# Attention scores as three float32r products from tile 4 on, and tile 1's probabilities split in float16

## The chip, the cores and the metric

The kernel runs on one core of a Trainium2 chip. The metric is the device time of one execution in microseconds (us); the kernel before takes 676.44 us, the median of three runs (675.19 to 678.43).

## What is computed

Attention with rotary embedding over 4 batches, 8 heads, 576 positions and head size 64, and then a two-layer network on the 2304 resulting rows of 512. All arrays are float32.

```python
q_rot, k_rot = rotate(q), rotate(k)
scores = matmul(q_rot, k_rot.T) / sqrt(64)
attn = exp(scores - max(scores))
attn = attn / (sum(attn) + 1e-09)
x = matmul(attn, v)                      # to [2304, 512]
h = x @ w_in                             # w_in [512, 2048]
g = maximum(h, 0) + alpha * minimum(h, 0)
out = g @ w_out                          # w_out [2048, 512]
```

## The kernel before, in words

The 2304 rows are cut into 18 tiles of 128 rows. 576 is four and a half tiles, so tile 4 and tile 13 hold the end of one batch and the start of the next, and each of these two is worked as two halves of 64 rows; the 16 others are whole. Two tiles make a block; there are nine blocks. Heads are worked in pairs (4 pairs a tile), since two heads of 64 fill the 128 partitions. The second layer stage that a block goes through is called an expert here: 16 steps j, each of a first-layer product of 128 columns of `w_in` (`l1`, into the buffer `h`), a leaky relu in two instructions (ACT, then DVE: the tile `r`) and a second-layer product (`l2`).

For a pair of heads, `pair` (L624) issues the scores on TensorE (PE) into two PSUM buffers, `pair`. Whole tiles use the two halves of the PE array, rows 0 to 63 for one head and 64 to 127 for the other. `half_pair` (L650) handles the two split tiles: it puts both heads' queries on a diagonal, `qd`, and uses the whole array. Then `head` (L680) takes the row maximum on DVE (`mx`), the exponential with its sum on ACT (`e`), and goes one of two ways:

- tiles 0 and 1 (`t < PRM["pf"]`, which is 2): `head_f32` (L733) turns the probabilities on PE with products by the identity (L745), copies them out of PSUM and multiplies by v in float32 (L751).
- all others: the probabilities are split into a float16 high part (`pp`, on ACT L707 or DVE) and a float16 rest (DVE L716), both are transposed by a DMA on the SP queue (L720, `pt<-pp`), and 14 float16 products follow (L727).

`keys` (L381) and `queries` (L602) load and rotate: a product with a table and a sum on POOL or DVE, into `ks` and `qn`. The weights come as 64-bit words. `weights` loads them on the SP queue into `wraw` (L529), and DVE turns each of 16 chunks into float32 by three instructions (L511, L516, L520). Blocks 0 and 1 run the expert in float32 (L817, L843); from block 2 on the first layer is three float16 products (L823) and the second three float32r products of split operands (L861).

The program writes nothing in the order of execution. Each operation is put in a list with a priority, its possible engines and a cost for each, and `Plan.run` deals the list out to the five engines ahead of time; the order, the engine and the buffers that come out of it are fixed in the program. The table `PRM` holds the offsets of the priorities. Each engine then works its instructions strictly in that order. SP's queue holds all loads and all DMA transposes, so an instruction there that waits holds up those behind it.

Of the kernel before, what the change touches and what calls it, by code (L numbers as in the profile page):

```python
# [9 lines left out]
F32 = mybir.dt.float32  # L10
F32R = mybir.dt.float32r
# [3 lines left out]
ACTF = mybir.ActivationFunctionType  # L15
# [36 lines left out]
class Tag:  # L52
    def __init__(self, pool, bufs, shape, dt, name, tag=None):
        self.pool, self.bufs, self.all, self.opened = pool, bufs, [], 0
        self.make = lambda: pool.tile(shape, dt, name=name, tag=f"{tag or name}{self.opened % bufs}")

    def new(self):
        k = len(self.all)
# [182 lines left out]
def attention_moe(ctx: ExitStack, tc: tile.TileContext, q, k, v, w_in, w_out, alpha, tab, eye, out):  # L241
# [64 lines left out]
    ks_T = tag("ks", PRM["nks"], [128, S], F32)  # L306
# [4 lines left out]
    qn_T = tag("qn", 2, [128, NP, 128], F32)  # L311
    st_T = tag("st", 2, [128, NP], F32)
    e_T = tag("e", 2, [128, S], F32)
    pp_T = tag("pp", 3, [128, 2, S], F16)
# [61 lines left out]
        small(at, lambda: nc.vector.reciprocal(out=dst(), in_=dst()), writes=[dst_acc])  # L376


    ks = {}

    def keys(at, b, p):  # L381
        r, t = rk_T.new(), ks_T.new()
        ks[b, p] = t
# [8 lines left out]
        op(at - PRM["ka"], {POOL: t_pool(S), DVE: (t_dve(S), slow)},  # L392
           lambda e: ENG[e].tensor_tensor(out=t(), in0=r()[:, 0], in1=r()[:, 1], op=ALU.add),
           reads=[(r, 0), (r, 1)], writes=[t])

# [204 lines left out]
    qs = {}  # L600

    def queries(at, t):  # L602
        raw, qn = qr_T.new(), qn_T.new()
        qs[t] = qn
        parts = tiles[t]
        cuts = [[0], [2]] if t == 0 else [[0, 2]]
        op(at - (PRM["qd0"] if t == 0 else PRM["qd"]), {SP: t_dma(128 * 2 * NP * 128 * 4)}, lambda e: nc.sync.dma_start(out=raw(), in_=q[t]),
           writes=[(raw, (p[2], x)) for p in parts for x in (0, 2)])
        for n, xs in enumerate(cuts):
            c, w = slice(xs[0], xs[-1] + 2), 2 * len(xs) * 128  # L610
            late = at - PRM["qa"] + 0.1 * n
            for b, s, a, z in parts:
                m = w * (z - a) // 128
                op(late, {POOL: t_pool(2 * m), DVE: (t_dve(2 * m), PRM["qr"])},
                   lambda e, s=s, a=a, z=z, c=c: ENG[e].tensor_tensor(
                       out=raw()[:, :, c, a:z], in0=raw()[:, :, c, a:z],
                       in1=tab_b()[:, :, s:s + z - a].unsqueeze(2).to_broadcast([128, 2, c.stop - c.start, z - a]),
                       op=ALU.mult),
                   reads=[tab_b], writes=[(raw, (a, x)) for x in xs])
            op(late, {POOL: t_pool(w), DVE: (t_dve(w), PRM["qr"])},  # L620
               lambda e, c=c: ENG[e].tensor_tensor(out=qn()[:, c], in0=raw()[:, 0, c], in1=raw()[:, 1, c], op=ALU.add),
               reads=[(raw, (p[2], x)) for p in parts for x in xs], writes=[(qn, x) for x in xs])


    sums, ys, xss, vos, xt = {}, {}, {}, {}, {}

    def pair(at, step, t, b, p, a, z, banks):
        kt, vt, qn = ks[b, p], vv[b, p], qs[t]
        if z - a < 128:
            return half_pair(at, t, b, p, a, z, banks[p % 2])  # L630
        ps = [x.new() for x in banks]


        def scores(e):
# [5 lines left out]
        op(at, {PE: PRM["tqk"]}, scores, kind=WIDE, reads=[(qn, p // 2 * 2), kt], writes=ps)  # L640
# [7 lines left out]
    qds, sts = {}, {}  # L648

    def half_pair(at, t, b, p, a, z, bank):  # L650
        kt, vt, qn = ks[b, p], vv[b, p], qs[t]
        if (t, a) not in qds:
            qd, sts[t, a] = qr_T.new(), st_T.new()
            qds[t, a] = qd
            for h in range(2):
                o, c = 64 * h, 64 - 64 * h
                op(at - 2, {POOL: 420, DVE: (t_dve(256, fast=True), 1)},
                   lambda e, o=o, c=c: ENG[e].memset(qd()[o:o + 64, 0, :, c:c + 64], 0.0), writes=[(qd, h)])
                op(at - 2, {ACT: t_act(256)},
                   lambda e, o=o: nc.scalar.activation(out=qd()[o:o + 64, 0, :, o:o + 64], in_=qn()[o:o + 64, :, a:z], func=ACTF.Copy),  # L660
                   reads=[(qn, 0), (qn, 2)], writes=[(qd, 2 + h)])
# [367 lines left out]
```

## Time and profile before

| what | value |
|---|---|
| median of 3 runs | 676.44 us (675.19, 676.44, 678.43) |
| span of the profiled execution | 674.6 us |
| PE busy | 643.3 us, 95% of the span |
| DVE busy | 471.6 us, 70% |
| ACT busy | 338.5 us, 50% |
| POOL busy | 218.7 us, 32% |
| the chain that ended last | PE 85%, DMA 7%, DVE 4%, ACT 2%, issue 1% |

The profile is of one execution. The page gives its span, from the first instruction to the last, and no other time for it; the median of the timed runs is 1.8 us above the span, so a change of the span is laid onto the median as it is. Busy shares are averages over stages that differ: in the first 54 us tile 0 is attended, from 54 to 92 us tile 1, from 92 to 166 us the float32 expert of block 0 runs with tiles 2 and 3, and from about 250 us on the split experts run. In timelines, L12 is line 12 of the kernel and "x8" is a number of merged instructions. A float32 product shows as two PE instructions, so the four score products of a pair are eight.

### The profile page before, as it was taken

Reading aid. Unit: us, or ns where it says so; the run is one execution under the profiler, and the core shown is the slowest. Engines: PE = TensorE matmul, PEld = TensorE weight load, DVE = VectorE, ACT = ScalarE, POOL = GpSimd, SP = SyncE. Lnnn points to the kernel's source line nnn. Section 1 sums busy time; section 2 is a strip of 40 time slices with the busy share of each in tenths; the row PEclk is TensorE's granted clock in tenths of the full one; section 3 lists DMA queues with packets and bytes.
Section 4 is the critical chain, followed back from the end, with each engine's and each line's share of the span. In section 5 each row is a group of like instructions: output and inputs, shape, how many; then the busy total and the mean of one; then the engine's idle time right before and its main releaser. Section 6 shows DMA issues by size and latency. Waiting matters only on the chain.

```text
span 674.6 us, 13695 instructions
## 1 busy us (share of the span) xinstructions
PE 643.3 (95%) x5378; PEld 480.3 (71%) x5378; DVE 471.6 (70%) x754; ACT 338.5 (50%) x752; POOL 218.7 (32%) x178
## 2 busy tenths in 40 slices
PE   1998999999999999999989999999999999999997
PEld 1577766676666667777767777788777777778775
DVE  4889799875877767587759776777766665664332
ACT  4355357653646548445634555554555544543322
POOL 3793101103476636165514221123233232211000
PEclk9999999999999999999979999999999999999999
DMA  8962885866674545658686646674865546553000
GB/s 292 329 245 97 307 249 125 195 105 149 162 201 88 121 82 120 121 137 189 148 170 116 120 87 80 114 163 93 153 129 102 88 75 102 107 100 52 32 0 32
DMA packets 185840, 90.69 MB, mean 134 GB/s; under 512 B 168624, under 2 KB 172848, under 8 KB 185776
## 3 DMA queue, kind: packets, MB, share of 16 engines
q1 hardware_dynamic: 185776, 89.82, 58.8%
q8 instruction: 42, 0.69, 0.4%
q14 instruction: 22, 0.18, 0.1%
HBM read 41.56 MB, written 4.72 MB: 69 GB/s over the span
## 4 chain that ended last, share of the span: by engine, by line
PE 85%; DMA 7%; DVE 4%; ACT 2%; issue 1%; SPq 1%; POOL 0%; ACTq 0%; DVEq 0%
PE pair L861 22%; PE h L823 21%; PE pair L638 10%; PE v L727 8%; PE h L817 8%; PE pair L843 7%; DMA pt<-pp 4%; PE pair L745 3%; PE v L751 2%; DMA kraw<-in_k_dram 2%; PE pair L666 2%; PE pair L468 1%; DVE mx L690 1%; DMA qr<-in_q_dram 1%; DMA xt<-xs 1%
## 5 line engine op out<-in xcount | busy, mean ns | idle before, releaser
L823 PE MATMUL h<-xt,wi 128*128 128x256 f16 x1344 | 175.7, 275 | 1.1 <-DMA xt<-xs 0.7
L823 PEld LDWEIGHTS <-wi 128*128 128x128 f16 x1344 | 120.1, 98 | 43.0 <-issue 28.5
L699 ACT ACTIVATE e<-pair,mx 128x576 f32<-128x576 f32 x144 | 105.8, 738 | 83.0 <-DVE mx L690 81.8
L837 DVE SCALAR_TENSOR_TENSOR r<-r,beta,h 128x256 f32<-128x256 f32 x144 | 68.8, 478 | 94.1 <-ACT r L834 93.0
L834 ACT ACTIVATE r<-h 128x256 f32<-128x256 f32 x144 | 55.2, 383 | 145.2 <-PE h L823 106.7
L690 DVE TENSOR_REDUCE mx<-pair 128x1 f32<-128x576 f32 x144 | 103.3, 751 | 25.6 <-PE pair L638 21.9
L854 POOL TENSOR_TENSOR gl<-r,gh 128x256 fp32r<-128x256 f32 x69 | 56.4, 818 | 175.6 <-ACT gh L851 152.9
L716 DVE SCALAR_TENSOR_TENSOR pp<-e,pp 128x576 f16<-128x576 f32 x128 | 102.6, 811 | 11.2 <-ACT pp L707 9.5
L861 PE MATMUL pair<-wh,gh 128*128 128x512 f32 x224 | 97.0, 433 | 0.0
L861 PE MATMUL pair<-wh,gl 128*128 128x512 f32 x224 | 88.6, 395 | 0.0
L727 PEld LDWEIGHTS <-pt 128*128 128x128 f16 (+1 forms) x2016 | 71.9, 102 | 23.0 <-issue 12.3
L861 PE MATMUL pair<-wo,gh 128*128 128x512 f32 x224 | 87.7, 391 | 0.0
L727 PE MATMUL v<-vv,pt 128*128 128x64 f16 (+1 forms) x2016 | 78.1, 195 | 4.6 <-DMA pt<-pp 4.6
L638 PE MATMUL pair<-ks,qn 64*128 64x288 f32 x512 | 82.3, 433 | 0.0
L851 ACT ACTIVATE gh<-r 128x256 fp32r<-128x256 f32 x102 | 42.5, 417 | 52.0 <-DVE r L837 26.7
L817 PE MATMUL h<-xt,wi 128*128 128x256 f32 x256 | 66.7, 392 | 1.3 <-DVE xt L788 1.2
L638 PEld LDWEIGHTS pair<-ks,qn 64*128 64x128 f32 x512 | 46.9, 189 | 23.7 <-issue 12.1
L843 PE MATMUL pair<-wo,r 128*128 128x512 f32 x128 | 60.5, 598 | 0.0
L817 PEld LDWEIGHTS h<-xt,wi 128*128 128x128 f32 x256 | 45.7, 190 | 14.9 <-issue 5.4
L707 ACT ACTIVATE pp<-e 128x576 f16<-128x576 f32 x76 | 51.4, 679 | 1.0
L861 PEld LDWEIGHTS pair<-wh,gh 128*128 128x128 f32 x224 | 42.2, 188 | 11.6 <-issue 3.1
L861 PEld LDWEIGHTS pair<-wh,gl 128*128 128x128 f32 x224 | 42.0, 187 | 10.4
(96 smaller groups left out, 715.6 us busy)
## 6 DMA issues: line engine op xcount, KB each, us to landing
kraw<-in_k_dram SPq DMA_DIRECT2D x16, 576.0 KB, 5.0
qr<-in_q_dram SPq DMA_DIRECT2D x18, 512.0 KB, 4.1
wraw<-in_moe_w_in_dram SPq DMA_DIRECT2D x16, 512.0 KB, 4.9
wraw<-in_moe_w_out_dram SPq DMA_DIRECT2D x16, 512.0 KB, 5.5
vraw<-in_v_dram SPq DMA_DIRECT2D x16, 320.0 KB, 4.1
out_dram<-os SPq DMA_DIRECT2D x18, 256.0 KB, 2.4
vv<-vv SPq DMA_DIRECT2D x32, 64.0 KB, 2.1
pt<-pp SPq DMA_TRANSPOSE x128, 3.3
```

What stands on the lines that cost most here:

```text
L638: nc.tensor.matmul(out=ps[h]()[:, x, :HS], lhsT=qn()[r, p], rhs=kt()[r, x * HS:(x + 1) * HS], start=True, stop=True)
L690: lambda e: nc.vector.tensor_reduce(out=mx()[a:z], in_=ps()[a:z, :, :HS], axis=AX.XY, op=ALU.max, negate=True),
L699: lambda e: nc.scalar.activation(out=ex()[a:z].rearrange("p (x c) -> p x c", x=2), in_=ps()[a:z, :, :HS], func=ACTF.Exp, bias=mx()[a:z], a ...
L716: lambda e: nc.vector.scalar_tensor_tensor(out=pp()[a:z, 1], in0=ex()[a:z], scalar=E_SC, in1=pp()[a:z, 0], op0=ALU.mult, op1=ALU.subtract),
L727: nc.tensor.matmul(out=v_b()[c:d, 2 * p + g], lhsT=pt()[:, s, o:o + d - c], rhs=vt()[:, g, w], start=(n == 0), stop=(n == len(order) - 1))
L817: nc.tensor.matmul(out=ps(), lhsT=w32(kk, j // FG)[:, f], rhs=x()[:, kk], start=(kk == 0), stop=(kk == KC - 1))
L823: nc.tensor.matmul(out=ps(), lhsT=wi_b()[:, kk, j // FG, w, f], rhs=x()[:, y * KC + kk], start=(kk == 0 and n == 0), stop=(kk == KC - 1 an ...
L834: lambda e: nc.scalar.activation(out=g(), in_=ps(), func=ACTF.Relu, scale=-1.0),
L837: lambda e: nc.vector.scalar_tensor_tensor(out=g(), in0=g(), scalar=beta_b()[:, j:j + 1], in1=ps(), op0=ALU.mult, op1=ALU.add),
L843: nc.tensor.matmul(out=po()[:, x], lhsT=g()[:, x * 128:(x + 1) * 128], rhs=wf[j // 2]()[:, j % 2], start=(j == 0), stop=(j == KF - 1))
L854: lambda e: ENG[e].tensor_tensor(out=gl(), in0=g(), in1=gh().bitcast(F32), op=ALU.subtract),
L861: nc.tensor.matmul(out=po()[:, x], lhsT=s()[:, ts], rhs=w, start=(j == 0 and c == 0), stop=(j == KF - 1 and c == 2))
```

## The change

- Scores from tile 4 on (`PRM["sf"]` is 4): keys and queries are split into a float32r high part and a float32r rest (`in_two`: one copy on ACT or DVE, one subtraction on POOL or DVE), and each score product becomes three float32r products (high by high, low by high, high by low) that add up in PSUM. A pair has 12 products in place of 4, a half pair 6 in place of 2. Tiles 0 to 3 keep the float32 scores; the names there are now `ks`, `qp`.
- `pf` goes from 2 to 1: tile 1's probabilities take the float16 way with the DMA transpose.
- `PRM` has new numbers throughout, so the order of all engines is new. A DMA scratch size is set to 512.

```diff
-PRM = {"pf": 2, "pc": 3.0, "si": 3.47, "sd": 7.38, "qd": 8.0, ...
+PRM = {"pf": 1, "pc": 3.12, "si": 9.73, "sd": 0.95, "qd": 6.72, ... "sf": 4, ...
...
+    def in_two(at, acc, src, dst, n, first, second):
+        op(at, {ACT: t_act(n), DVE: (t_dve(n, fast=True), PRM[first])},
+           lambda e: nc.scalar.activation(out=dst()[:, 0], in_=src(), func=ACTF.Copy) if e == ACT
+           else nc.vector.tensor_copy(out=dst()[:, 0], in_=src()), reads=acc[0], writes=acc[1])
+        op(at, {POOL: t_pool(n), DVE: (t_dve(n), PRM[second])},
+           lambda e: ENG[e].tensor_tensor(out=dst()[:, 1], in0=src(), in1=dst()[:, 0].bitcast(F32), op=ALU.subtract),
+           reads=acc[0] + acc[1], writes=acc[2])
...
+    TERMS = ((0, 0), (1, 0), (0, 1))
...
         def scores(e):
             for x in range(2):
-                for h in range(2):
-                    r = slice(64 * h, 64 * h + 64)
-                    nc.tensor.matmul(out=ps[h]()[:, x, :HS], lhsT=qn()[r, p], rhs=kt()[r, x * HS:(x + 1) * HS], start=True, stop=True)
+                for n, (i, j) in enumerate(TERMS if split else [(0, 0)]):
+                    for h in range(2):
+                        r, c = slice(64 * h, 64 * h + 64), slice(x * HS, (x + 1) * HS)
+                        nc.tensor.matmul(
+                            out=ps[h]()[:, x, :HS], lhsT=qn()[r, i, p] if split else qn()[r, p],
+                            rhs=kt()[r, j, c] if split else kt()[r, c], start=(n == 0), stop=(n == 2 or not split))
...
+                for n, (i, j) in enumerate(TERMS):
+                    nc.tensor.matmul(out=ps()[:, x, :HS], lhsT=qd()[:, i, p], rhs=kt()[:, j, x * HS:(x + 1) * HS],
+                                     start=(n == 0), stop=(n == 2))
...
+                if t >= PRM["sf"] and (b, p) not in kh:
+                    split_keys(at, b, p)
```

The order on DVE while tile 1 is attended. First before, from the third pair of tile 1 on (`mx<-pair_603`); `wo<-wraw` and its like are the conversions of weights:

```order
L690 TENSOR_REDUCE mx<-pair_603 128x1
L690 TENSOR_REDUCE mx<-pair_605 128x1
L511 TENSOR_SCALAR wo<-wraw 128x1024
L516 SCALAR_TENSOR_TENSOR wo<-wraw,wo 128x1024
L520 SCALAR_TENSOR_TENSOR wo<-wraw,wo 128x1024
L422 TENSOR_REDUCE wm<-vraw 128x1
```

And the change, from the same pair of tile 1 (`mx<-pair_565`) to the next:

```order
L737 TENSOR_REDUCE mx<-pair_565 128x1
L737 TENSOR_REDUCE mx<-pair_567 128x1
L547 SCALAR_TENSOR_TENSOR wi<-wraw,wi 128x2x512
L543 SCALAR_TENSOR_TENSOR wo<-wraw,wo 128x1024
L763 SCALAR_TENSOR_TENSOR pp<-e,pp 128x576 x2
L737 TENSOR_REDUCE mx<-pair_621 128x1
L737 TENSOR_REDUCE mx<-pair_623 128x1
```

Each pair of tile 1 now has two `pp<-e,pp` on DVE between the maxima, and fewer conversions stand between two pairs.

The order on DVE just ahead of the first leaky relu of block 0's expert (`r<-r,beta,h`), before:

```order
L771 TENSOR_TENSOR y<-v,rs 128x512
L511 TENSOR_SCALAR wi<-wraw 128x2x512
L690 TENSOR_REDUCE mx<-pair_721 128x1
L690 TENSOR_REDUCE mx<-pair_723 128x1
L788 COPY xt<-v 128x4x128
L516 SCALAR_TENSOR_TENSOR wi<-wraw,wi 128x2x512
L716 SCALAR_TENSOR_TENSOR pp<-e,pp 128x576 x2
L837 SCALAR_TENSOR_TENSOR r<-r,beta,h 128x256
```

And in the change, where `pair_741` and `pair_814` are the second and third pair of tile 2:

```order
L737 TENSOR_REDUCE mx<-pair_741 128x1
L737 TENSOR_REDUCE mx<-pair_743 128x1
L818 TENSOR_TENSOR y<-v,rs 128x512
L547 SCALAR_TENSOR_TENSOR wo<-wraw,wo 128x1024
L763 SCALAR_TENSOR_TENSOR pp<-e,pp 128x576 x2
L538 TENSOR_SCALAR wo<-wraw 128x1024
L452 TENSOR_REDUCE cm<-wm 128x1
L543 SCALAR_TENSOR_TENSOR wo<-wraw,wo 128x1024
L547 SCALAR_TENSOR_TENSOR wo<-wraw,wo 128x1024
L737 TENSOR_REDUCE mx<-pair_814 128x1
L737 TENSOR_REDUCE mx<-pair_816 128x1
L355 TENSOR_SCALAR pp<-e 128x576
```

Two more pairs of tile 2 stand ahead of that relu than before (three in place of one).

The order on the SP queue around the first DMA transpose (`pt<-pp`), before and in the change:

```order
L529 DMA wraw<-in_moe_w_out_dram 128x512 x2
L412 DMA vraw<-in_v_dram 128x640
L529 DMA wraw<-in_moe_w_in_dram 128x512
L529 DMA wraw<-in_moe_w_out_dram 128x512
L720 DMA_TRANSPOSE pt<-pp 128x9x128 x2
L529 DMA wraw<-in_moe_w_in_dram 128x512 x2
```

```order
L556 DMA wraw<-in_moe_w_in_dram 128x512
L439 DMA vraw<-in_v_dram 128x640
L767 DMA_TRANSPOSE pt<-pp 128x9x128 x8
L556 DMA wraw<-in_moe_w_out_dram 128x512
L767 DMA_TRANSPOSE pt<-pp 128x9x128
L556 DMA wraw<-in_moe_w_out_dram 128x512
```

Of the 32 weight loads, 24 stood ahead of the first transpose and 12 do now; the others alternate with transposes.

## Rows read from the trace of the kernel before

**Rows 1.** The page, part 1: busy time of each engine, share of the span, instructions

```profile
PE 643.3 (95%) x5378; PEld 480.3 (71%) x5378; DVE 471.6 (70%) x754; ACT 338.5 (50%) x752; POOL 218.7 (32%) x178
```

**Rows 2.** Busy per stage: us, PE, PEld, DVE, ACT, POOL, then clock, DMA, GB/s

```profile
54.00:92.00 38.00, 34.05 (x236) 27.58 (x237) 32.30 (x41) 16.59 (x35) 6.49 (x6) 1.00 0.59 206
92.00:166.00 74.00, 73.87 (x536) 50.06 (x536) 58.93 (x90) 43.74 (x93) 10.80 (x11) 1.00 0.72 154
...
320.00:360.00 40.00, 36.83 (x334) 28.23 (x331) 29.38 (x53) 20.81 (x49) 14.95 (x13) 0.91 0.73 154
```

**Rows 3.** Timeline of PE, one pair of tile 1: start, us, what

```profile
64.85 2.97 PE L745 MATMUL pair<-eye,e 128*128 128x128 f32 x20 [1.08 <-ACT e L699]
67.76 1.35 PE L751 MATMUL v<-vraw,pt 128*128 128x64 f32 x9
...
70.18 1.47 PE L751 MATMUL v<-vraw,pt 128*128 128x64 f32 x10
72.09 2.97 PE L745 MATMUL pair<-eye,e 128*128 128x128 f32 x20 [0.45 <-ACT e L699]
```

**Rows 4.** What DVE waited for from 54 to 91 us: total, times, longest

```profile
DVE mx L690 <- PE pair L638: 3.3, 2, 2.0
DVE y L771 <- PE v L751: 2.0, 2, 1.7
```

**Rows 5.** Timeline of DVE, tile 1's first maximum to the first leaky relu

```profile
54.26 0.74 DVE L690 TENSOR_REDUCE mx<-pair 128x1 f32<-128x576 f32 x1
...
70.36 1.42 DVE L690 TENSOR_REDUCE mx<-pair 128x1 f32<-128x576 f32 x2 [1.33 <-PE pair L638]
71.69 0.68 DVE L511 TENSOR_SCALAR wo<-wraw 128x1024 int32<-128x1024 int32 x1
72.41 1.23 DVE L516 SCALAR_TENSOR_TENSOR wo<-wraw,wo 128x1024 int32<-128x1024 int32 x1
73.67 1.22 DVE L520 SCALAR_TENSOR_TENSOR wo<-wraw,wo 128x1024 int32<-128x1024 int32 x1
...
85.13 0.69 DVE L771 TENSOR_TENSOR y<-v,rs 128x512 f32<-128x512 f32 x1 [1.68 <-PE v L751]
...
89.40 1.42 DVE L716 SCALAR_TENSOR_TENSOR pp<-e,pp 128x576 f16<-128x576 f32 x2
90.85 0.48 DVE L837 SCALAR_TENSOR_TENSOR r<-r,beta,h 128x256 f32<-128x256 f32 x1
```

**Rows 6.** Timeline of PE: a score pair, float32r products, a head's float16 products

```profile
299.89 1.24 PE L638 MATMUL pair<-ks,qn 64*128 64x288 f32 x8
301.06 0.50 PE L861 MATMUL pair<-wh,gh 128*128 128x512 f32 x1
301.40 0.39 PE L861 MATMUL pair<-wo,gh 128*128 128x512 f32 x1
301.63 0.40 PE L861 MATMUL pair<-wh,gl 128*128 128x512 f32 x1
...
302.57 0.58 PE L727 MATMUL v<-vv,pt 128*128 128x64 f16 x14
302.99 0.82 PE L823 MATMUL h<-xt,wi 128*128 128x256 f16 x6
```

**Rows 7.** Timeline of PE in two narrow windows inside that score pair

```profile
300.24 0.41 PE L638 MATMUL pair<-ks,qn 64*128 64x288 f32 x2
...
300.48 0.41 PE L638 MATMUL pair<-ks,qn 64*128 64x288 f32 x2
```

**Rows 8.** Timeline of PE's weight loads: the score pair's first four, float32r's first two

```profile
299.89 0.30 PEld L638 LDWEIGHTS pair<-ks,qn 64*128 64x128 f32 x4 [0.21 <-issue]
...
301.06 0.19 PEld L861 LDWEIGHTS pair<-wh,gh 128*128 128x128 f32 x1 [0.39 <-issue]
301.17 0.19 PEld L861 LDWEIGHTS pair<-wo,gh 128*128 128x128 f32 x1
```

**Rows 9.** Timeline of PE: the longest wait of the later stages

```profile
347.62 0.93 PE L727 MATMUL v<-vv,pt 128*128 128x64 f16 x14 [2.87 <-DMA pt<-pp]
```

**Rows 10.** Page, part 6: issues, KB each, us to landing

```profile
wraw<-in_moe_w_out_dram SPq DMA_DIRECT2D x16, 512.0 KB, 5.5
```

More of the change, by code (lines that the diff above doesn't have):

```diff
@@ L54, in __init__ @@
         self.pool, self.bufs, self.all, self.opened = pool, bufs, [], 0
-        self.make = lambda: pool.tile(shape, dt, name=name, tag=f"{tag or name}{self.opened % bufs}")
+        self.name = tag or name
+        self.make = lambda: pool.tile(shape, dt, name=name, tag=f"{self.name}{self.opened % bufs}")
     def new(self):
@@ L305, in attention_moe @@
     wo_pool = ctx.enter_context(tc.tile_pool(name="wo_p", bufs=1))
-    ks_T = tag("ks", PRM["nks"], [128, S], F32)
+    kh_T = tag("kh", PRM["nks"], [128, 2, S], F32R)
     vv_T = tag("vv", PRM["nvv"], [128, 2, NSEG + NH, D], F16)
@@ L310, in attention_moe @@
     qr_T = tag("qr", 2, [128, 2, NP, 128], F32)
-    qn_T = tag("qn", 2, [128, NP, 128], F32)
+    qn_T = tag("qn", 2, [128, 2, NP, 128], F32R)
     st_T = tag("st", 2, [128, NP], F32)
@@ L376, in scale_of, with plain @@
         small(at, lambda: nc.vector.reciprocal(out=dst(), in_=dst()), writes=[dst_acc])
-    ks = {}
+    ks, kh = {}, {}
+    def plain(pool_tag, buf, shape, name):
+        buf.make = lambda: pool_tag.pool.tile(shape, F32, name=name, tag=f"{pool_tag.name}{pool_tag.opened % pool_tag.bufs}")
+        return buf
+    def in_two(at, acc, src, dst, n, first, second):
[5 more added lines that the diff above has]
+           reads=acc[0] + acc[1], writes=acc[2])
     def keys(at, b, p):
-        r, t = rk_T.new(), ks_T.new()
-        ks[b, p] = t
+        r = rk_T.new()
         op(at - PRM["kl"], {SP: t_dma(128 * 2 * S * 4)}, lambda e: nc.sync.dma_start(out=r(), in_=k[b, p]),
@@ L391, in keys, with split_keys @@
                reads=[tab_b], writes=[(r, y) for y in x])
-        op(at - PRM["ka"], {POOL: t_pool(S), DVE: (t_dve(S), slow)},
-           lambda e: ENG[e].tensor_tensor(out=t(), in0=r()[:, 0], in1=r()[:, 1], op=ALU.add),
-           reads=[(r, 0), (r, 1)], writes=[t])
+        if b == 0:
+            t = ks[b, p] = plain(kh_T, kh_T.new(), [128, S], "ks")
+            out, acc = t, [t]
+        else:
+            out, acc = lambda: r()[:, 0], [(r, 0)]
+            ks[b, p] = (out, acc)
+        op(at - PRM["ka"], {POOL: t_pool(S), DVE: (t_dve(S), slow)},
+           lambda e: ENG[e].tensor_tensor(out=out(), in0=r()[:, 0], in1=r()[:, 1], op=ALU.add),
+           reads=[(r, 1)] if b else [(r, 0), (r, 1)], writes=acc)
+        if b == 0:
+            ks[b, p] = t
+    def split_keys(at, b, p):
+        t = kh[b, p] = kh_T.new()
+        src, acc = ks[b, p] if b else (ks[b, p], [ks[b, p]])
+        in_two(at - PRM["kt0" if b == 0 else "kt"], (acc, [(t, 0)], [(t, 1)]), src, t, S, "khd", "kld")
     vv, vraw, vs, xu = {}, {}, {}, {}
@@ L602, in queries @@
     def queries(at, t):
+        split = t >= PRM["sf"]
         raw, qn = qr_T.new(), qn_T.new()
+        if not split:
+            plain(qn_T, qn, [128, NP, 128], "qp")
         qs[t] = qn
@@ L619, in queries @@
                    reads=[tab_b], writes=[(raw, (a, x)) for x in xs])
+            to = (lambda c=c: raw()[:, 0, c]) if split else (lambda c=c: qn()[:, c])
+            acc = [(raw, (p[2], x)) for p in parts for x in xs]
             op(late, {POOL: t_pool(w), DVE: (t_dve(w), PRM["qr"])},
-               lambda e, c=c: ENG[e].tensor_tensor(out=qn()[:, c], in0=raw()[:, 0, c], in1=raw()[:, 1, c], op=ALU.add),
-               reads=[(raw, (p[2], x)) for p in parts for x in xs], writes=[(qn, x) for x in xs])
+               lambda e, c=c, to=to: ENG[e].tensor_tensor(out=to(), in0=raw()[:, 0, c], in1=raw()[:, 1, c], op=ALU.add),
+               reads=[] if split else acc, writes=acc if split else [(qn, x) for x in xs])
+        if split:
+            acc = [(raw, (p[2], x)) for p in parts for x in (0, 2)]
+            in_two(at - PRM["qt"], (acc, [(qn, 0)], [(qn, 1)]), lambda: raw()[:, 0], qn, NP * 128, "qhd", "qld")
     sums, ys, xss, vos, xt = {}, {}, {}, {}, {}
+    TERMS = ((0, 0), (1, 0), (0, 1))
     def pair(at, step, t, b, p, a, z, banks):
-        kt, vt, qn = ks[b, p], vv[b, p], qs[t]
+        vt, qn = vv[b, p], qs[t]
         if z - a < 128:
@@ L631, in pair @@
         ps = [x.new() for x in banks]
+        split = t >= PRM["sf"]
+        kt = kh[b, p] if split else ks[b, p]
         def scores(e):
             for x in range(2):
-                for h in range(2):
-                    r = slice(64 * h, 64 * h + 64)
-                    nc.tensor.matmul(out=ps[h]()[:, x, :HS], lhsT=qn()[r, p], rhs=kt()[r, x * HS:(x + 1) * HS], start=True, stop=True)
-        op(at, {PE: PRM["tqk"]}, scores, kind=WIDE, reads=[(qn, p // 2 * 2), kt], writes=ps)
+                for n, (i, j) in enumerate(TERMS if split else [(0, 0)]):
[4 more added lines that the diff above has]
+                            rhs=kt()[r, j, c] if split else kt()[r, c], start=(n == 0), stop=(n == 2 or not split))
+        op(at, {PE: PRM["tqs" if split else "tqk"]}, scores, kind=WIDE,
+           reads=[(qn, 0), (qn, 1), (kt, 0), (kt, 1)] if split else [(qn, p // 2 * 2), kt], writes=ps)
         for h in range(2):
@@ L650, in half_pair @@
     def half_pair(at, t, b, p, a, z, bank):
-        kt, vt, qn = ks[b, p], vv[b, p], qs[t]
+        kt, vt, qn = kh[b, p], vv[b, p], qs[t]
         if (t, a) not in qds:
             qd, sts[t, a] = qr_T.new(), st_T.new()
+            qd.make = lambda: qr_T.pool.tile([128, 2, NP, 128], F32R, name="qd", tag=f"{qr_T.name}{qr_T.opened % qr_T.bufs}")
             qds[t, a] = qd
@@ L656, in half_pair @@
                 o, c = 64 * h, 64 - 64 * h
[L657 to L661, printed above, removed]
+                op(at - 2, {POOL: 840, DVE: (t_dve(512, fast=True), 1)},
+                   lambda e, o=o, c=c: ENG[e].memset(qd()[o:o + 64, :, :, c:c + 64].bitcast(F32), 0.0), writes=[(qd, h)])
+                op(at - 2, {ACT: t_act(512)},
+                   lambda e, o=o: nc.scalar.activation(
+                       out=qd()[o:o + 64, :, :, o:o + 64], in_=qn()[o:o + 64, :, :, a:z].bitcast(F32), func=ACTF.Copy),
+                   reads=[(qn, 0), (qn, 1)], writes=[(qd, 2 + h)])
         qd, ps = qds[t, a], bank.new()
@@ L665, in scores @@
             for x in range(2):
-                nc.tensor.matmul(out=ps()[:, x, :HS], lhsT=qd()[:, 0, p], rhs=kt()[:, x * HS:(x + 1) * HS], start=True, stop=True)
-        op(at, {PE: 980}, scores, kind=WIDE, reads=[(qd, x) for x in range(4)] + [kt], writes=[ps])
+                for n, (i, j) in enumerate(TERMS):
+                    nc.tensor.matmul(out=ps()[:, x, :HS], lhsT=qd()[:, i, p], rhs=kt()[:, j, x * HS:(x + 1) * HS],
+                                     start=(n == 0), stop=(n == 2))
+        op(at, {PE: PRM["tqh"]}, scores, kind=WIDE, reads=[(qd, x) for x in range(4)] + [(kt, 0), (kt, 1)], writes=[ps])
         head(at, t, b, p, None, a, z, ps, vt)
@@ L1014 @@
     laid = _lay_out(inputs)
-    nc = _bacc.Bacc("TRN2", target_bir_lowering=False, num_devices=1)
+    nc = _bacc.Bacc("TRN2", target_bir_lowering=False, num_devices=1, dynamic_dma_scratch_size=512)
     arrays, args = {}, []
```

2 lines of the change are left out of this document (1 added, 1 removed).

## The prediction

> **What bounds the kernel now.** I read the page first: PE is busy 95% of the span and no other engine above 70% [rows 1]. An average over stages says little about a change in two of them, so the second view is the busy time by stage [rows 2]. From 92 us on PE has no room: 73.87 of 74 us. From 54 to 92 us, where tile 1 is attended, PE is busy 34.05 of 38 us and DVE 32.30: two engines are close to full there, and the reader should keep that in mind, since the change takes PE's work out of exactly that stage and gives some to DVE. The view of DVE's waits says who led: its maxima waited 3.3 us for PE's scores and its `y` 2.0 us for PE's products [rows 4]. So PE is the bound of tile 1's stage by some 5 us only, and of everything behind it by far more.
>
> **The scores.** Per whole pair, now: PE starts the scores at 299.89 and the next product at 301.06 [rows 6], a slot of 1.17 us. Inside it two instructions start together every 0.24 us, one for each half of the array [rows 7]; four such steps are 0.97, and 0.20 goes into the first weight load and the change back. After the change each half runs six float32r products of 288 columns. No row has one of this shape. The nearest is the second layer's, 512 columns, which starts every 0.23 us (301.40, 301.63) [rows 6]; by columns that is 0.234 × 288 / 512 = 0.131 us (five steps from 301.40 to 302.57 make 0.234 each). The lower bound is the next weight load: two of them follow at 0.11 us [rows 8]. The upper bound: if the 0.02 us by which 0.234 exceeds 512 columns at the full clock, 2.4 GHz, is a fixed cost, a product takes 0.12 + 0.02 = 0.14. I take 0.131, since it is the same kind of product. Six are 0.79 against 0.97: 0.18 less, with the 0.20 unchanged. There are 12 whole tiles from tile 4 on, 48 pairs, and 16 half pairs, whose two float32 products I take as four steps of 0.24 too. In all 64 × 0.18 = 11.6 us less on PE (8 to 19 by the bounds), and all of it lies where PE is the bound.
>
> What else it issues: 16 splits of keys and 14 of queries, one copy on ACT (most of them) and one subtraction on POOL. ACT and POOL stand at 50% and 32% [rows 1], and the plan puts the splits ahead of their use, so I price them at nothing. If a split were late, PE's next scores would wait, and behind them everything in PE's order. The weights of a score product are a different part of the queries for each of the three, but the second pair of loads already goes ahead under the first products: four loads have started 0.30 us after the first, while the first products last until 300.24 and beyond [rows 7, 8].
>
> By the Trainium skill's page "TensorE: Matmul & The Clock Gate", section "Back-to-back issue gap", a product of N columns would take N/2.4 + 2.5 ns, so 122 ns here and an estimate of 15 us saved; the float32r rows of this trace are slower than that formula for 512 columns, so I stay with the row.
>
> **Tile 1.** PE loses, per pair, the turns (64.85 to 67.76: 2.91 us) and two heads' products (1.25 and 1.47) [rows 3]: 5.6 us, 22.5 for four pairs. It gains 8 heads of 14 float16 products at 0.42 us (302.57 to 302.99) [rows 6], 3.4 us. PE has 19.1 us less to do. Were PE the bound, all of this would be saved. It isn't any more. DVE works strictly in order, so I add up what stands in its order between tile 1's first maximum (at 54.26, with the same work ahead of it on PE and DVE but one product with the table) and the first leaky relu of the expert, which began at 90.85 [rows 5]. In the change that is 7 pairs of maxima at 1.42 us (four of tile 1, three of tile 2), 9.9; 13 rest instructions at 0.71, 9.2; of the conversions 4 first steps at 0.72 (71.69 to 72.41) and 8 later ones at 1.2 (1.26 and about 1.14), 12.5; six others of about 0.7 as the `y` (two `y`, two of v's maxima, two casts), 4.2, and three small ones, 0.6. The sum is 36.4 us. With 1 us of waiting (before it was 5.3 [rows 4], all for PE, which is no longer late) the relu begins at 54.3 + 36.4 + 1 = 91.7 us, 0.9 later than before. **So tile 1's 19.1 us come back almost entirely as PE waiting for DVE.** What remains is that two more pairs of tile 2 are already scored by then (2 × 1.26) and one pair's products done (2 × 0.42): 3.4 us that PE need not do later. Behind the relu DVE has room again (58.93 of 74 [rows 2]) and PE is the bound.
>
> ACT does the exponentials of the two more pairs and most casts in that stage, but no longer the copies of the turned probabilities; at 16.59 of 38 us [rows 2] it hides them. The SP queue matters: 8 transposes now stand ahead of 20 of the 32 weight loads. A load lands 5.5 us after issue [rows 10], and between the issue behind the first transpose of tile 2 and DVE's next first step stand some 6 us of DVE work by the prices above; if it lands late, DVE stops, and with it the maxima that PE waits for. I price that at 0 to 4 us.
>
> **The sum.** 674.6 + 0.9 − 3.4 − 11.6 = 660.5 us of span; with the 1.8 us between span and median, 662. Other stalls go or come with the new order: the one of 2.87 us on a transpose at 347.62 also brought a stretch at half clock (0.91 mean over 40 us [rows 2, 9], so 7 us at 1.2 GHz, some 3.5 lost). Nothing in the change removes its cause, so I leave it, with ±5 us for such events.
>
> **The rivals.**
> *The whole cut comes through.* DVE's list would have to be worth 20 us less, or PE would find other work while it waits. PE's order is fixed too, and the expert's first product stands behind three pairs of tile 2, which speaks against; for it speaks that DVE had 5.3 us idle. 674.6 − 19.1 − 11.6 + 1.8 = 646. Chance 0.2.
> *Scores at par.* If a float32r product on half the array takes 0.162 us, six cost what four steps do now, and 662 + 11.6 = 674. The rows at 0.23 for 512 columns speak against. Chance 0.1.
> *A slow start.* Loads behind transposes hold DVE for 4 us beyond the 1 us taken, and PE, idle for half of tile 1's stage, falls to half clock as at 347 us (3.5): 662 + 7.5 = 669 to 672. The clock held at 1.00 there before [rows 2], but with 15 us more work on PE. Chance 0.14.
> *Slower.* The loads of the six products in one half of the array don't hide under its products. Each then costs load plus product, 0.11 + 0.131, six 1.45 against 0.97: 64 × 0.48 = 30.6 us more in place of 11.6 less, and 662 + 11.6 + 30.6 = 704. It decides against the kernel from a pair's slot of about 1.4 us on. Against it: the score pair's loads already overlap within a half, since two steps follow at 0.24 us with a load each [rows 7, 8]. For it: those are float32, and each lasts twice as long. Chance 0.04. The Trainium skill has this rule on the page "TensorE: Matmul & The Clock Gate", section "The mechanism": loads overlap products in flight only when the row group differs. The float32 rows here disagree, so its chance stays small.
> That the change doesn't do what it says is excluded by the order: tile 1's transposes and the new products are there.
>
> **How the numbers follow.** The forecast, 662, has 0.52; the rivals 0.2, 0.1, 0.14 and 0.04. A measurement of this kernel tells a difference of about 0.5%, 3.4 us. The range 646 to 672 takes in the forecast with its ±8, the whole cut and the slow start; it leaves out scores at par, the slower case and a little below. Faster than 673 are the forecast, the whole cut, most of the slow start and half of scores at par: 0.89. Same 0.07, slower 0.04.
>
> **What would show it.** The scores' slot should be 0.99 us and their steps 0.13. In tile 1's stage DVE should be busy over 90%, with PE waiting for it, and the first leaky relu begin between 89 and 97 us. If it begins near 75 us the DVE sum is wrong, and if a pair's slot is 1.17 or more the price of the float32r product is.

## The result and the profile after

The changed kernel takes 668.09 us, median of 6 runs (666.67 to 673.45); the kernel before took 677.62 us in the 6 runs beside it (675.19 to 679.98). The ratio is 0.9877 [0.9843, 0.9911]: 1.2% faster. The forecast was 662, the range 646 to 672. The profiled execution is one of 668.09 us with a span of 666.3 us, so the 1.8 us between the two are as before.

The page of the changed kernel, busy time of each engine and, from its second part, TensorE's clock in 40 slices:

```profile
PE 626.2 (94%) x5554; PEld 478.8 (72%) x5554; DVE 490.0 (74%) x745; ACT 362.4 (54%) x796; POOL 273.2 (41%) x210
...
PEclk9988689999999999999999999999999999999999
```

Beside [rows 1] PE lost 17.1 us, DVE gained 18.4, ACT 23.9 and POOL 54.5. The clock line has a 6 in its fifth slice, where there was none before. The stages show more. Columns as in [rows 2]: length, busy of PE, PEld, DVE, ACT and POOL, granted clock, DMA share, GB/s:

```profile
54.00:92.00 38.00, 29.22 (x235) 21.06 (x235) 34.58 (x48) 19.64 (x42) 7.17 (x6) 0.73 0.76 165
92.00:166.00 74.00, 72.52 (x492) 50.39 (x491) 68.11 (x94) 48.45 (x101) 26.72 (x18) 1.00 0.82 214
...
320.00:360.00 40.00, 37.56 (x367) 29.58 (x368) 34.31 (x53) 23.81 (x55) 19.89 (x17) 1.00 0.72 156
```

In tile 1's stage PE is busy 29 us in place of 34 and DVE 34.6 in place of 32.3, and the granted clock is 0.73 in place of 1.00. At 320 to 360 us the clock is 1.00: the stretch at half clock behind the wait of [rows 9] is gone.

**The scores.** PE's timeline, one whole pair of the changed kernel, and three narrow windows inside another pair:

```profile
566.21 1.06 PE L678 MATMUL pair<-kh,qn 64*128 64x288 f32 x12
567.21 0.58 PE L774 MATMUL v<-vv,pt 128*128 128x64 f16 x14
...
300.10 0.43 PE L678 MATMUL pair<-kh,qn 64*128 64x288 f32 x4
300.23 0.43 PE L678 MATMUL pair<-kh,qn 64*128 64x288 f32 x4
300.36 0.43 PE L678 MATMUL pair<-kh,qn 64*128 64x288 f32 x4
```

The pair's slot is 567.21 − 566.21 = 1.00 us, where it was 1.17 [rows 6], and a step takes 0.13 us.

**Tile 1.** DVE's timeline from tile 1's first maximum to the expert's first leaky relu (L884):

```profile
55.84 1.42 DVE L737 TENSOR_REDUCE mx<-pair 128x1 f32<-128x576 f32 x2 [1.30 <-PE pair L678]
57.24 0.69 DVE L818 TENSOR_TENSOR y<-v,rs 128x512 f32<-128x512 f32 x1
58.36 1.61 DVE L538 TENSOR_SCALAR wi<-wraw 128x1024 int32<-128x1024 int32 x1 [0.43 <-DMA wraw<-in_moe_w_in_dram]
...
94.06 0.47 DVE L884 SCALAR_TENSOR_TENSOR r<-r,beta,h 128x256 f32<-128x256 f32 x1
```

The first maximum came at 55.84 in place of 54.26, the relu at 94.06 in place of 90.85 [rows 5]: tile 1's 19 us are not there. PE now waits in that stage, from 54 to 92 us, mostly for exponentials (total, times, longest); ACT's exponentials in turn wait 11.1 us there, in six places, for maxima on DVE:

```profile
PE pair L678 <- ACT e L746: 6.0, 3, 3.8
PE v L831 <- DVE y L818: 2.8, 1, 2.8
```

**Behind the relu.** One window from the relu to the end, first of the kernel before, then of the changed one:

```profile
90.85:674.60 583.75, 573.44 (x4934) 426.56 (x4932) 401.50 (x674) 297.49 (x673) 176.32 (x150) 0.99 0.57 116
```

```profile
94.06:666.30 572.24, 560.09 (x5100) 430.65 (x5096) 420.30 (x655) 315.81 (x704) 232.43 (x181) 1.00 0.60 124
```

So the whole gain lies here: 583.75 − 572.24 = 11.5 us, of which 13.4 is less busy time on PE and −1.8 more idle time. Not all of the 13.4 is less work: in the trace before, PE stood at 0.50 of the full clock from 346.85 to 350.85 us and at 0.66 in the next 4 us, the stretch behind the wait of [rows 9], and that it is gone gives back an estimated 3 us (half of 3.23 us busy, and 0.34 of 4.00). What PE waits for there, from 94 us on:

```profile
PE v L774 <- DMA pt<-pp: 2.7, 3, 1.5
PE h L870 <- DVE r L884: 2.1, 3, 1.3
PE h L864 <- DVE r L884: 1.3, 1, 1.3
PE pair L908 <- POOL gl L901: 1.0, 1, 1.0
```

Waits for DVE's relu come to 3.4 us, where the same view of the kernel before has 0.4, and the 1.0 for POOL's `gl` is new; those for transposes fell from 4.6 to 2.7.

### The profile page after: what moved, and what is told of

It reads as the page before. It is cut to its first block, busy times and chain, and to the rows that moved or that the text cites. A ratio compares the mean times of both kernels' runs of the same rounds, so it can differ in the third digit from the quotient of the medians.

```text
span 666.3 us, 14118 instructions
## 1 busy us (share of the span) xinstructions
PE 626.2 (94%) x5554; PEld 478.8 (72%) x5554; DVE 490.0 (74%) x745; ACT 362.4 (54%) x796; POOL 273.2 (41%) x210
## 4 chain that ended last, share of the span: by engine, by line
PE 79%; DMA 10%; DVE 7%; ACT 2%; issue 1%; SPq 1%; POOL 1%; ACTq 0%; DVEq 0%; POOLq 0%
PE pair L908 22%; PE h L870 21%; PE v L774 9%; PE h L864 8%; PE pair L678 8%; PE pair L890 8%; DMA pt<-pp 5%; PE pair L712 2%; DMA kraw<-in_k_dram 2%; DVE pp L763 2%; DVE mx L737 1%; DMA qr<-in_q_dram 1%; PE pair L792 1%; DMA wraw<-in_moe_w_in_dram 1%; DVE vv L476 1%
## 5 line engine op out<-in xcount | busy, mean ns | idle before, releaser
L870 PE MATMUL h<-xt,wi 128*128 128x256 f16 x1344 | 167.9, 273 | 2.2 <-DVE r L884 2.1
L870 PEld LDWEIGHTS <-wi 128*128 128x128 f16 x1344 | 122.5, 98 | 36.6 <-issue 23.2
L763 DVE SCALAR_TENSOR_TENSOR pp<-e,pp 128x576 f16<-128x576 f32 x136 | 129.4, 959 | 20.2 <-ACT pp L754 19.0
L901 POOL TENSOR_TENSOR gl<-r,gh 128x256 fp32r<-128x256 f32 x67 | 58.5, 873 | 162.9 <-ACT gh L898 78.8
L884 DVE SCALAR_TENSOR_TENSOR r<-r,beta,h 128x256 f32<-128x256 f32 x144 | 68.7, 477 | 74.1 <-ACT r L881 72.7
L774 PEld LDWEIGHTS <-pt 128*128 128x128 f16 (+1 forms) x2128 | 76.9, 103 | 30.0 <-issue 22.1
L774 PE MATMUL v<-vv,pt 128*128 128x64 f16 (+1 forms) x2128 | 87.4, 196 | 2.7 <-DMA pt<-pp 2.7
L754 ACT ACTIVATE pp<-e 128x576 f16<-128x576 f32 x89 | 60.1, 681 | 24.6 <-DMA pt<-pp 19.6
L864 PE MATMUL h<-xt,wi 128*128 128x256 f32 x256 | 64.1, 389 | 1.3 <-DVE r L884 1.3
L678 PE MATMUL pair<-kh,qn 64*128 64x288 f32 x576 | 51.2, 309 | 0.0
L678 PEld LDWEIGHTS pair<-kh,qn 64*128 64x128 f32 x576 | 39.9, 184 | 13.2 <-issue 8.5
```

Source lines behind the costliest of these rows:

```text
L678: nc.tensor.matmul(out=ps[h]()[:, x, :HS], lhsT=qn()[r, i, p] if split else qn()[r, p], rhs=kt()[r, j, c] if split else kt()[r, c], start= ...
L754: lambda e: nc.scalar.activation(out=pp()[a:z, 0], in_=ex()[a:z], func=ACTF.Copy, scale=1.0 if early else E_SC) if e == ACT
L763: lambda e: nc.vector.scalar_tensor_tensor(out=pp()[a:z, 1], in0=ex()[a:z], scalar=E_SC, in1=pp()[a:z, 0], op0=ALU.mult, op1=ALU.subtract),
L774: nc.tensor.matmul(out=v_b()[c:d, 2 * p + g], lhsT=pt()[:, s, o:o + d - c], rhs=vt()[:, g, w], start=(n == 0), stop=(n == len(order) - 1))
L864: nc.tensor.matmul(out=ps(), lhsT=w32(kk, j // FG)[:, f], rhs=x()[:, kk], start=(kk == 0), stop=(kk == KC - 1))
L870: nc.tensor.matmul(out=ps(), lhsT=wi_b()[:, kk, j // FG, w, f], rhs=x()[:, y * KC + kk], start=(kk == 0 and n == 0), stop=(kk == KC - 1 an ...
```

## The experiments

The theory: the scores give the gain, and tile 1 gives nothing, because DVE's in-order list holds the first relu. All but three of the kernels below keep the changed kernel's order and alter only what an instruction does or which engine does it, or add products inside an existing step. Each was timed beside the kernel before; since that one's median differed each time (677.62 to 682.96), ratios are compared first.

**Scores back to the old price.** Four float32 products of the high parts per pair in place of twelve, and two per half pair in place of six, with the splits left in. The products with the rests are left out.

```diff
-                for n, (i, j) in enumerate(TERMS if split else [(0, 0)]):
...
+                        out=ps[h]()[:, x, :HS], lhsT=qn()[r, 0, p].bitcast(F32) if split else qn()[r, p],
+                        rhs=kt()[r, 0, c].bitcast(F32) if split else kt()[r, c], start=True, stop=True)
```

> Order of every engine as in the changed kernel; from tile 4 on each pair again runs 4 float32 products (a half pair 2) in place of 12 (6) float32r ones. It leaves out the two low terms (high by high alone is computed), the splits stay. Theory (PE is the bound behind tile 1's stage, so the scores' gain comes through whole): a pair's slot goes back from 0.99 to 1.17 us, a half pair's from about 0.88 to 0.97, 48 x 0.18 + 16 x 0.09 = 10 us slower than the changed kernel, so about 678 us, the kernel before's time. Rival (the gain is mostly swallowed by waits, the changed kernel is faster through its new order): under 671 us.

Measured: 679.02 us (676.17 to 685.65), ratio 1.0001 [0.996, 1.0042]; a pair's slot is 1.18 us again. The gain is gone. Against 0.9877 that is 1.24%, 8.4 us; by the medians 679.02 − 668.09 = 10.9. The new scores are worth 8 to 11 us (some 5 to 12 by the two intervals), and all the rest, tile 1, the splits and the new order together, comes to nothing that the interval of ±0.4% (some 3 us) would show. It doesn't follow that each of them is nothing by itself.

**A part alone, planned anew.** Three kernels: the changed one with `pf` back at 2 (tile 1 in float32, under the new table); the changed one with `pf` 2 and the old table's numbers (the scores alone); the kernel before with `pf` 1 (tile 1 alone, under the old table).

```diff
-PRM = {"pf": 1, ...
+PRM = {"pf": 2, ...
```

> The changed kernel with pf back at 2: tile 1 turned and multiplied in float32 on PE again, the order dealt out anew with the changed table. Theory (tile 1's 19 us of PE work come back as waiting, so the way that tile 1 goes matters little): 664 to 672 us. Rival (tile 1's change carries the gain and the new order hides it): 680 us or more.

> The split scores alone: pf 2, the numbers of the table of before for all that before has, and the changed kernel's numbers for the new ones. Theory (the scores carry the gain): 10 us less than before, a ratio of 0.985, with the first leaky relu at 91 to 92 us. Rival (the gain needs the new order or tile 1): a ratio of 0.995 or more.

> The kernel before with pf at 1 and nothing else: tile 1's probabilities split in float16 and turned by DMA, float32 scores throughout. Theory (DVE, the clock and the transposes take the place of PE in tile 1's stage): within 4 us of before, a ratio of 0.994 to 1.006. Rival (the whole 19 us come through): a ratio of 0.975 or less.

Measured, in this order: 694.84 us, ratio 1.0205 [1.0129, 1.0281]; 695.01, 1.0224 [1.0158, 1.029]; 702.39, 1.0331 [1.026, 1.0401]. All three are slower than the kernel before, and all three miss the theory's numbers. The first two lie on the side of their rivals (680 us or more; 0.995 or more), so that by the numbers alone tile 1's change, or the order, would carry the gain. The traces show where the time goes. With tile 1 in float32 under the new table, the first relu comes at 114.72 us, 20.7 later than in the changed kernel, so most of the loss lies in tile 1's own stage, where the stretch from 62 to 94 us reads (columns as above):

```profile
62.00:94.00 32.00, 28.38 (x115) 22.66 (x115) 17.69 (x20) 9.15 (x19) 0.00 (x0) 0.52 0.56 201
```

And one of PE's turns in it, in PE's timeline:

```profile
74.41 5.32 PE L792 MATMUL pair<-eye,e 128*128 128x128 f32 x20 [1.77 <-ACT e L746]
```

PE is at half clock, and the turns take 5.32 us in place of 2.97 [rows 3]; before, with the same turns in another order, the clock was 1.00 [rows 2]. The scores alone under the old table lose most behind the first relu (600.3 us from there to the end, where the kernel before takes 583.75), among other places at 172 us and after, where the plan puts a split of queries and other work in DVE's list between a relu and the next (DVE's timeline):

```profile
174.90 2.93 DVE L393 TENSOR_TENSOR qn<-qr,qn 128x512 fp32r<-128x512 f32 x1
...
179.63 0.47 DVE L884 SCALAR_TENSOR_TENSOR r<-r,beta,h 128x256 f32<-128x256 f32 x1
```

Tile 1 alone under the old table has its first relu at 96.12, 5.3 us later than before, and loses 22.7 us more behind it, among other places to loads that come late (the chain of waits, 172 to 215 us):

```profile
175.22 5.59 DMA kraw<-in_k_dram
...
202.06 7.04 DMA qr<-in_q_dram
```

What follows: a table of priorities belongs to the set of operations it was made for. A part planned again under a table made for others measures the order with it, 2.0 to 3.3% or 14 to 22 us here, and the part can't be told from it. The worth of the scores is told here by the kernel with a fixed order alone; what tile 1's change is worth apart from the order, no run shows.

**Tile 1's rests on POOL.** If DVE's list is the bound, 8 rests (8 × 0.71) off it should bring the relu forward. For tile 1 the factor in `pp` is dropped, as the subtraction used on POOL has none.

```diff
-               lambda e: nc.vector.scalar_tensor_tensor(
+               lambda e: nc.gpsimd.tensor_tensor(out=pp()[a:z, 1], in0=ex()[a:z], in1=pp()[a:z, 0], op=ALU.subtract) if t == 1
+               else nc.vector.scalar_tensor_tensor(
```

> Order as in the changed kernel, but tile 1's 8 rest instructions (0.71 us each on DVE) run on POOL at the same place, without the factor 16, which tile 1's casts and normalisation drop too. Theory (DVE's list bounds tile 1's stage): 8 x 0.71 = 5.7 us less on DVE, the first leaky relu begins about 5 us earlier than 94.1 us and the kernel takes about 663 us. Rival (PE at half clock and the chain scores - maximum - exponential - scores bound it): relu at 93 us or later, 667 us or more.

Measured: 667.8 us, ratio 0.9812 [0.9763, 0.9861], the first relu at 94.75. No gain: 5 us less was expected. DVE's groups from 55 to 95 us (busy, mean ns of one), first of the changed kernel, then of this one:

```profile
L543 DVE SCALAR_TENSOR_TENSOR wi<-wraw,wi 128x1024 int32<-128x1024 int32 x1 | 1.2, 1209 | 0.0
L538 DVE TENSOR_SCALAR wo<-wraw 128x1024 int32<-128x1024 int32 x3 | 2.1, 684 | 0.0
L737 DVE TENSOR_REDUCE mx<-pair 128x1 f32<-128x576 f32 x14 | 9.9, 745 | 1.3 <-PE pair L678 1.3
```

```profile
L543 DVE SCALAR_TENSOR_TENSOR wi<-wraw,wi 128x1024 int32<-128x1024 int32 x1 | 2.2, 2179 | 0.0
L538 DVE TENSOR_SCALAR wo<-wraw 128x1024 int32<-128x1024 int32 x3 | 4.2, 1401 | 0.0
L737 DVE TENSOR_REDUCE mx<-pair 128x1 f32<-128x576 f32 x14 | 9.9, 749 | 2.0 <-PE pair L678 2.0
```

And POOL's rests in the same view:

```profile
L763 POOL TENSOR_TENSOR pp<-e,pp 128x576 f16<-128x576 f32 x8 | 13.0, 1642 | 3.2 <-ACT pp L754 3.1
```

The conversions stretch to about twice their time while POOL works, and the maxima, which read PSUM, do not. DVE lost 5.7 us of rests and gained nearly as much in conversions (18.1 us in place of 13.5, all their groups in the two views): its busy time between first maximum and relu is 35.8 us in both kernels. The Trainium skill, page "GPSIMD Engine Reference", section "8. Key points", says that POOL shares its SBUF interfaces with VectorE and contends with DVE instructions in a two-port mode or with two SBUF inputs. This trace agrees as far as it goes: L543 has two SBUF inputs (1209 to 2179 ns) and the maxima none (745 and 749). L538 has one, at nearly twice L543's speed, and stretches too (684 to 1401); that it is in such a mode no row shows.

**Keeping the clock up.** Two float32 products of 256 columns into an unused buffer behind each of tile 1's eight heads; then the same with the rests on POOL.

```diff
+            if t == 1:
+                for _ in range(2):
+                    nc.tensor.matmul(out=warm[0](), lhsT=eye_b(), rhs=tab_b()[:, 0, :256], start=True, stop=True)
```

> Order as in the changed kernel; after each of tile 1's 8 heads PE runs two products more into an unused buffer (float32, 128 x 256, 0.43 us each way at the full clock), which keep it busier in tile 1's stage. They compute nothing that is used. Theory (DVE bounds the stage, the half clock costs little there): the clock stays at 1.00 or nearly so, the first leaky relu begins 0 to 2 us earlier than at 94.1, 666 to 668 us. Rival (the half clock is what holds the stage): relu at 89 us or earlier, 660 to 663 us.

> Both: tile 1's rests on POOL and the additional products on PE, order as in the changed kernel. Theory: as with the rests on POOL alone, plus what the clock gives once DVE's list is shorter: relu at 86 to 89 us, 660 to 663 us. Rival (half clock alone counts): the same time as with the additional products alone.

Measured: 664.75 us (663.05 to 669.1), ratio 0.9771 [0.9717, 0.9825], and 665.07, 0.9778 [0.9727, 0.9828]. The first relu comes at 91.43 with the products alone, between theory and rival; with the rests on POOL it stays at 94.20, where 86 to 89 was expected. Since the changed kernel had been timed apart from these, it was run again as it is, beside the first of these two and one that also issues four such products behind tile 0's turn:

> The changed kernel once more, as the one to compare with on the same chip: 664 to 672 us by every theory, the first leaky relu at 94 to 96 us, with the clock at half for some 20 us between 60 and 92.

> The kernel with two additional products after each of tile 1's heads, once more beside the changed kernel. Theory (the half clock in tile 1's stage costs 2 to 3 us): 2 to 5 us less than the changed kernel on the same chip. Rival (the difference seen between two jobs was the chip's): within 1 us of it.

> The same with four more products after tile 0's turn, where the clock still fell at 61.7 us while PE waited 2.5 us for the exponentials. Theory (each stretch at half clock costs in the stage): no half clock from 25 us on, 1 to 2 us less than with the fewer products. Rival (what is left is held by DVE and the transposes): the same time within 1 us.

Measured: 667.85 us, 0.9847 [0.98, 0.9894]; 666.35, 0.9812 [0.9772, 0.9852]; 669.47, 0.9856 [0.9812, 0.99]. The stretch from 54 to 94 us in this order:

```profile
54.00:94.00 40.00, 31.06 (x254) 22.07 (x251) 36.95 (x52) 21.84 (x47) 7.39 (x6) 0.74 0.82 176
```

```profile
54.00:94.00 40.00, 32.01 (x284) 22.66 (x282) 36.45 (x50) 21.78 (x47) 6.72 (x6) 0.91 0.78 177
```

```profile
54.00:94.00 40.00, 33.73 (x301) 23.77 (x300) 37.56 (x52) 22.11 (x48) 8.45 (x6) 1.00 0.79 181
```

The clock goes from 0.74 to 0.91 and 1.00, and the time hardly follows: 1.5 us less than the changed kernel and then 1.6 us more than it, with intervals that overlap. The second lies between its theory's 2 to 5 us and its rival's 1; the further 1 to 2 us of the third are not there. From first maximum to relu the changed kernel takes 38.2 and 38.1 us in its two traces, the kernel with two products 36.8 and 38.6 in its two, the third 37.2. Two traces of one kernel differ by up to 1.8 us, so half clock costs tile 1's stage some 1 us by these traces, and nothing isn't excluded. With the clock at 1.00 throughout, DVE is busy 36.0 us of the 37.16 between first maximum and relu: what PE loses by half clock there, it would mostly have waited. Behind the relu the third kernel takes 573.9 us in place of 572.2.

**DVE's list cut short.** The two added products per head stay, and the eight rests replaced by zeros that ACT writes. The low part of tile 1's probabilities is left out.

```diff
-               lambda e: nc.vector.scalar_tensor_tensor(
+               lambda e: nc.scalar.activation(out=pp()[a:z, 1], in_=ex()[a:z], func=ACTF.Copy, scale=0.0) if t == 1
+               else nc.vector.scalar_tensor_tensor(
```

> The kernel with additional products on PE, and tile 1's 8 rest instructions taken off DVE without giving them to POOL: ACT writes zeros in the place of the rest (0.68 us each on ACT). It leaves out the low part of tile 1's probabilities. Theory (with the clock held, DVE's list is next): the relu begins 3 to 5 us earlier than at 91.5 us, about 661 us. Rival (the transposes and the three buffers of pp hold the stage): the relu at 90 us or later, 664 us or more.

Measured: 666.73 us (663.38 to 668.12), ratio 0.9799 [0.9742, 0.9856]; relu at 93.21. From first maximum to relu it takes 38.35 us, as long as the changed kernel, though DVE is busy only 30.1 us of them, 5.7 less, and idle 8.3 in place of 2.5. The theory that DVE's list alone is the bound falls. The chain of waits of that stage (start, us, what):

```profile
64.89 3.47 DMA pt<-pp
...
70.83 3.29 DMA pt<-pp
...
75.48 3.22 DMA pt<-pp
...
85.68 5.80 DMA pt<-pp
```

Between them ACT writes `pp` (L754): there are three `pp` buffers, a transpose holds one for 3.2 to 5.8 us, and ACT can't write the next until one is free: it waited 5.0 us, in five places, for a transpose, against 1.7 us, once, in the changed kernel. The zeros also add 5.0 us of work to ACT, so ACT isn't cleared as a part of this bound. A fourth buffer wasn't tried.

**Shorter transposes too.** As the kernel just told, with transposes of 5 in place of 9 blocks for tile 1, and without the four products per head that use the low part.

```diff
-           lambda e: nc.sync.dma_start_transpose(out=pt()[:, :NSEG, :z - a], ...
+           lambda e: nc.sync.dma_start_transpose(out=pt()[:, :NH if t == 1 else NSEG, :z - a], ...
```

> The kernel without tile 1's rests on DVE (ACT writes zeros), and its DMA transposes shortened from 9 to 5 blocks of 128 columns, with the four products of the low part's blocks left out: the low part of tile 1's probabilities is missing. With the rests alone gone the relu stayed at 93 us. Theory (DVE's list and the transposes hold the stage together, one taking over when the other is shortened): with both shortened the relu begins at 87 to 90 us, 658 to 662 us. Rival (something else, such as the loads of weights, holds it): the relu at 92 us or later, and no gain over the kernel without the rests.

Measured: 665.67 us (661.29 to 670.56), ratio 0.9771 [0.9726, 0.9817]; from first maximum to relu 36.6 us, 1.75 less than with the long ones, which is no more than two traces of one kernel differ by. The 658 to 662 us expected are not there: this is the rival's side, no clear gain over the kernel without the rests. The chain, in the slowest of the six runs, now has one transpose and two loads of weights:

```profile
56.04 7.65 DMA wraw<-in_moe_w_in_dram
...
82.22 2.65 DMA pt<-pp
...
85.59 5.47 DMA wraw<-in_moe_w_out_dram
```

By this one chain the next limit is the loads on the same queue. How much of the rest each of loads, ACT and a last stretch at half clock holds stays open.

## Why the prediction was right, and where it was off

The direction and the mechanism held: the scores pay, and what tile 1 takes off PE comes back as waiting. 668.1 lies in the range, 6 us above the forecast and just below the slow start's 669 to 672. Of the 6 us, 2.4 came by the first relu and 3.4 behind it; there, terms that the sum had wrong offset each other, so that the closeness is partly luck.

- **The step, right.** Forecast 0.131 us by columns, measured 0.13; slot 0.99, measured 1.00. The range of the saving is a little off: 0.11 us a step makes 64 × 0.31 = 20 us and not 19. The slower rival is out: a half's next load hides under its products, and the pair's six steps would have taken 1.45 us otherwise. The Trainium skill, page "TensorE: Matmul & The Clock Gate", section "The mechanism", lets loads overlap only where the row group differs, though it also speaks of a background weight buffer; for these shapes the trace disagrees with the "only".
- **The half pairs, mis-sized.** "16 half pairs, whose two float32 products I take as four steps of 0.24 too". They use the whole array, no row of theirs was read, and they gave little: a half pair's slot went from 0.97 us (143.39 to 144.36) to 0.88 (439.79 to 440.67). PE's groups behind the relu, first before, then after (busy us, mean ns):

```profile
L666 PE MATMUL pair<-ks,qr 128*128 128x288 f32 x64 | 18.1, 407 | 0.0
```

```profile
L712 PE MATMUL pair<-kh,qd 128*128 128x288 f32 x96 | 16.9, 313 | 0.0
```

  1.2 us less in place of 16 × 0.18 = 2.9. With it the scores come to 48 × 0.17 + 1.2 = 9.4 us in place of 11.6, within the 8 to 11 of the experiment.
- **The first relu, right in kind and 2.4 us late.** Forecast 91.7, measured 94.06, inside the 89 to 97 given. DVE's list was priced well: 36.4 against 35.8 us busy. The rest is 1.6 us by which the first maximum came later, where I had allowed nothing, and 2.5 us of waiting where I took 1. The 1.6 us come from tile 0's stage: DVE's added product with the table stood ahead of a pair's maxima, PE waited 1.94 us for the exponentials, and the turn behind them ran partly at half clock (0.61 from 36 to 39 us). The same turn, first before, then after:

```profile
34.18 2.97 PE L745 MATMUL pair<-eye,e 128*128 128x128 f32 x20 [0.38 <-ACT e L699]
```

```profile
34.38 4.52 PE L792 MATMUL pair<-eye,e 128*128 128x128 f32 x20 [1.94 <-ACT e L746]
```

  In the second trace of the changed kernel that wait was 0.38 us, the clock stayed at 1.00 and the first maximum came at 55.11, so this term changes from run to run.
- **"DVE alone" was too narrow a cause.** The changed kernel's own chain of that stage already has one transpose, 5.20 us from 75.84. With 5.7 us less on DVE, transposes and their three buffers ended as late, and with shorter transposes, by one trace, the loads did. Three limits seem to lie within some 2 us of each other, so the whole cut, 646, was out of reach by more than DVE's order.
- **The slow start, its sign without its price.** PE did fall to half clock: in three stretches of the stage, by windows of the changed kernel.

```profile
62.00:73.00 11.00, 8.27 (x70) 5.97 (x70) 11.00 (x16) 6.79 (x15) 1.84 (x1) 0.53 0.60 113
...
76.00:83.00 7.00, 5.92 (x58) 4.30 (x54) 5.40 (x9) 2.81 (x6) 0.00 (x0) 0.52 1.01 164
...
86.00:90.00 4.00, 4.00 (x18) 2.71 (x18) 4.00 (x6) 1.78 (x4) 0.00 (x0) 0.57 0.79 194
```

  The rival priced this at 3.5 us; the kernels that hold the clock up show some 1 us in the stage, or nothing. DVE did not stop 4 us for a load either: the waits for `wraw` are 0.4 us. The condition came true, the cost did not.
- **Behind the relu.** Forecast 568.8 us of span (660.5 − 91.7), measured 572.2. The 3.4 us look like 1.7 of the half pairs' term and 1.8 of added idle time, the waits for `r` and `gl` above. But the forecast also left in the stall of [rows 9] with its half clock, since "Nothing in the change removes its cause", and both are gone: 2.87 us of waiting and an estimated 3 us of PE's time. Without them the sum would have been 562.9. The 9.3 us from there to 572.2 are the 1.7; some 0.5 of the whole pairs (48 × 0.01); 4.7 of new waits (1.8 + 2.87); and by what is left some 2.4 of PE's time, which no row here assigns. That the sum came within 3.4 us is luck. I had priced ACT's and POOL's splits and the new order at nothing; no wait for a split shows, but the relu and `gl` stand behind more work: DVE has 18.8 us more in that window than before, POOL 56.1.
- **The order priced at ±5.** For this order it held. That it can carry 14 to 22 us, the part-alone kernels show.

The lowest median, 664.75 us, is that of the kernel with two added products per head; run again it took 666.35. Beside the changed kernel on one chip that is 1.5 us less, within what the intervals leave open.

## What to carry to other kernels

When work leaves the bounding engine, add up the in-order list of the next engine between two events, as for the relu here; then do the same for the buffers and the queue, since a limit close behind the first takes over at once. Test a part by keeping the order and changing contents; a replanned part measures the plan. Price each shape from a row of its own: the half pairs' 0.97 us was in the trace before, without the 0.20 us that a whole pair loses, though their new price, 0.88, stood in no row.

## What the hardware showed that was not expected

- DVE and POOL slow each other: a conversion of 1024 elements took 2.18 us beside POOL's subtraction and 1.21 without it, and two of POOL's subtractions took 3.48 us beside conversions and 2.52 beside maxima (60.62 and 70.67 us in the trace with the rests on POOL). So POOL was no free place for 5.7 us of DVE work.
- PE fell to half clock in a stage in which it was busy 29 of 38 us; the first stretch began in a wait of 3.8 us that ended at 64.39. In the kernel with tile 1 in float32 it stood at 0.52 of the full clock for 32 us while busy 28.4 of them, the turns among it; half clock is 1.2 GHz, so it was there nearly throughout. Before the change the same float32 turns ran at 1.00. What made the difference isn't settled. In the changed kernel's stage the added products of float32 ended most of it.
- Half clock cost little where PE waits for others: from 0.74 to 1.00, tile 1's stage was shorter by 1 us, which is less than two traces of one kernel differ by. Where PE leads it costs more: tile 0's turn took 4.52 us in place of 2.97, and the maxima behind it came as much later.
